# Float64 words rounded in five VectorE operations instead of seven, four places for a row of sums, and x of the gates prepared ahead of w3 @ w_out

## The chip, the cores and the metric

One Trainium2 chip, one core. The number is device time in microseconds (us) of one execution of the whole program, as a median of runs. The engines of the core are TensorE (PE, matmuls), VectorE (DVE), ScalarE (ACT), GpSimd (POOL) and SyncE (SP), whose row issues nearly all transfers between the chip's memory and the core's SBUF. Each engine works through its own row of instructions in order.

## The reference

```python
# attention: B=4, H=8, S=576, D=64; k and v averaged over groups of 8 rows
scores = scale * (q @ k_p.T);  attn = softmax(scores);  x = attn @ v_p      # -> x: 2304 x 512
# experts: E=4, hidden size F=1024, p = normalized domain_probs
for e in range(4):
    out += p[:, e:e+1] * (relu(x @ w1[e]) @ w2[e])
# gates: x = out
h = ((x @ g1) * (x @ g2)) @ w3          # 512 -> 1024, 1024 -> 1024
return h @ w_out                        # 1024 -> 512, 2304 x 512 in fp32
```

All inputs come as float64 words in memory, so a value is a pair of 32-bit words.

## The kernel before

Products need more than one fp32 pass of TensorE, so each operand is kept as a high part (rounded to fp32r) and the low rest, and `mm3` does three matmuls for one product (L170 to L172: high x low, low x high, high x high). `hi_lo` makes the two parts: ACT writes the high one (L175), DVE or POOL subtracts (L176).

The work goes in stages: the attention and a lead (to about 40 us), expert 0 in units (to 279), experts 1 to 3 with four batches each of 576 tokens (to 871), the product w3 @ w_out (to 925), and the gated part (to 1205). Expert 0 runs in units of one block of 384 tokens and one chunk of 128 hidden columns: `expert_h` makes a hidden chunk (DVE at L665), `accumulate` multiplies a block's four sums by p (L680), and `weights_of(j)` (L742 to L745 and L176) prepares the weights of the next expert's hidden product j between them. `at_pairs` says at which unit each is called.

A batch of experts 1 to 3 (`batch`) has a hidden part, `hidden(j)` for j = 0 to 3, each of seven products (`seven`, a scheme of seven products for eight) of 288 columns into banks `s`, with sums on DVE at L925, and then a second product in two halves g = 0, 1 of eight steps k (one per hidden chunk, four `mm3` of 288 columns each; step = 8g + k). At the end of each half four multiplies on DVE (L1225, out of PSUM into `part`, times p as `pb`) and four adds on POOL (L1226, into `acc`) take the sums away. Between the steps other work is called: splits of the next expert's weights (`stream.split`), its `weights_of`, and `round_some(1)`. The PSUM banks are used in turn in a ring of eight (`bank_r`), so that the first product of the next batch needs a bank that the multiplies must have emptied.

`round_some` makes one step of `Rounding`: it takes 128 x 256 float64 words of a weight matrix of the later stages, rounds them to fp32 with integer operations (L270 to L277 on DVE, L278 on POOL) and stores the result in memory (buffers `gate`, `w`, `wo`; in the trace the tiles lie in the areas `x5h` and `x5l`). There are 80 such steps, which are done with the last batch of expert 3. The step's result tile has two places, so a step waits until the store of the one two before has gone.

The stage w3 @ w_out runs as 24 units of nine or six `mm3`'s matmuls (`w_units`, weights and hidden tiles in the areas `round` and `edge`, raw words loaded as `raw<-w`), at first inside g = 1 of the last batch of expert 3 (`W3_AHEAD`). Beside it the DVE and ACT prepare x for the first gated batch (`load_x`, `prepare_x`, L758 and L871 to L874), and `put_away` stores it (`kept<-xo`, L886) so that it can be loaded again for later use.

## Time and profile before

| | |
|---|---|
| median of 3 runs | 1205.94 us (1205.91 to 1206.03) |
| profiled execution | 1207.31 us, span 1205.6 us, mean granted clock 0.994 |
| PE busy | 1171.2 us, 97% of the span |
| DVE busy | 867.4 us, 72% |
| POOL busy | 515.0 us, 43% |
| ACT busy | 366.7 us, 30% |
| moved by DMA | 222.42 MB, 184 GB/s over the span |

The median is of whole executions; the profiled execution took 1207.31, and its span is what the trace covers. Times in rows are us from the start of the span. A row of the timeline gives start, duration, engine, line, operation, the names of output and inputs, the shape, and in brackets the idle time of the engine ahead of it with what ended it. A duration of a matmul is longer than the distance to the next, since they overlap.

### The profile page before, as it was taken

Reading aid. Unit: us, or ns where it says so; the run is one execution under the profiler, and the core shown is the slowest. Engines: PE = TensorE matmul, PEld = TensorE weight load, DVE = VectorE, ACT = ScalarE, POOL = GpSimd, SP = SyncE. Lnnn points to the kernel's source line nnn. Section 1 sums busy time; section 2 is a strip of 40 time slices with the busy share of each in tenths; the row PEclk is TensorE's granted clock in tenths of the full one; section 3 lists DMA queues with packets and bytes.
Section 4 is the critical chain, followed back from the end, with each engine's and each line's share of the span. In section 5 each row is a group of like instructions: output and inputs, shape, how many; then the busy total and the mean of one; then the engine's idle time right before and its main releaser. Section 6 shows DMA issues by size and latency. Waiting matters only on the chain.

```text
span 1205.6 us, 21677 instructions
## 1 busy us (share of the span) xinstructions
PE 1171.2 (97%) x7965; PEld 1125.8 (93%) x7965; DVE 867.4 (72%) x1841; ACT 366.7 (30%) x671; POOL 515.0 (43%) x559
## 2 busy tenths in 40 slices
PE   7999999999999998999999999999989999999998
PEld 6899999999999998999999999999967999999998
DVE  7776643657777987888888778777777777785454
ACT  4533332235132134421314423032344332331010
POOL 6965122355454446654545645345310222251121
PEclk9999999999999999999999999999999999999999
DMA  8856534546665863578574565575366344845641
GB/s 211 211 139 148 173 106 148 191 163 248 225 205 179 257 176 107 167 211 257 175 221 150 164 212 177 191 267 159 128 209 220 114 160 159 331 162 208 225 182 44
DMA packets 184494, 222.42 MB, mean 184 GB/s; under 512 B 55676, under 2 KB 127428, under 8 KB 184388
## 3 DMA queue, kind: packets, MB, share of 16 engines
q1 hardware_dynamic: 184388, 221.05, 57.3%
q8 instruction: 62, 1.02, 0.3%
q14 instruction: 44, 0.36, 0.1%
HBM read 149.13 MB, written 71.86 MB: 183 GB/s over the span
## 4 chain that ended last, share of the span: by engine, by line
PE 68%; DVE 12%; DMA 8%; issue 5%; POOL 4%; ACT 2%; SPq 1%; DVEq 0%; POOLq 0%; ACTq 0%
PE g L170 11%; PE g L171 11%; PE g L172 11%; PE s L170 11%; PE s L171 10%; PE s L172 10%; DMA raw<-in_moe_w_dram 2%; PE x_ps L520 1%; POOL plain L1226 1%; DMA gate<-x5l 1%; DVE plain L925 1%; PE sc L474 1%; DVE x5l L275 1%; DMA raw<-w 1%; PE at_ps L508 1%
## 5 line engine op out<-in xcount | busy, mean ns | idle before, releaser
L176 POOL TENSOR_TENSOR round<-plain,round 128x576 fp32r<-128x576 f32 x128 | 186.6, 1463 | 314.3 <-ACT round L175 290.0
L170 PE MATMUL g<-round,w2h 128*128 128x288 f32 (+1 forms) x960 | 292.7, 305 | 2.4 <-DVE plain L680 2.1
L171 PE MATMUL g<-round,w2l 128*128 128x288 f32 (+1 forms) x960 | 291.1, 303 | 0.0
L172 PE MATMUL g<-round,w2h 128*128 128x288 f32 (+1 forms) x960 | 291.1, 303 | 0.0
L170 PE MATMUL s<-xo,wh 128*128 128x288 f32 x840 | 249.8, 297 | 13.6 <-DVE s L1225 10.9
L172 PE MATMUL s<-xo,wh 128*128 128x288 f32 x840 | 248.6, 296 | 0.0
L171 PE MATMUL s<-xo,wl 128*128 128x288 f32 x840 | 248.1, 295 | 0.0
L170 PEld LDWEIGHTS g<-round,w2h 128*128 128x128 f32 x960 | 180.5, 188 | 3.8 <-DVE plain L680 2.4
L925 DVE TENSOR_TENSOR plain<-s,plain 128x288 f32<-128x288 f32 x320 | 134.0, 452 | 67.0 <-PE s L172 33.8
L171 PEld LDWEIGHTS g<-round,w2l 128*128 128x128 f32 x960 | 180.6, 188 | 0.0
L172 PEld LDWEIGHTS g<-round,w2h 128*128 128x128 f32 x960 | 180.6, 188 | 0.0
L170 PEld LDWEIGHTS s<-xo,wh 128*128 128x128 f32 x840 | 158.4, 189 | 15.9 <-DVE s L1225 12.3
L172 PEld LDWEIGHTS s<-xo,wh 128*128 128x128 f32 x840 | 158.5, 189 | 0.0
L171 PEld LDWEIGHTS s<-xo,wl 128*128 128x128 f32 x840 | 158.1, 188 | 0.2
L175 ACT ACTIVATE round<-plain 128x576 fp32r<-128x576 f32 x132 | 89.7, 682 | 161.8 <-DVE plain L1253 158.8
L278 POOL TENSOR_TENSOR x5l<-x5l 128x256 f32<-128x256 f32 x80 | 58.9, 736 | 173.6 <-DVE x5l L277 166.1
L1159 ACT ACTIVATE plain<-plain 128x576 f32<-128x576 f32 x96 | 65.3, 680 | 158.6 <-DVE plain L925 157.0
L927 ACT ACTIVATE plain<-s 128x288 f32<-128x288 f32 x80 | 31.7, 397 | 238.2 <-PE s L172 238.0
L925 DVE TENSOR_TENSOR plain<-s,pb 128x288 f32<-128x288 f32 x160 | 67.8, 455 | 15.5 <-PE s L172 5.8
L665 DVE SCALAR_TENSOR_TENSOR round<-g,round 128x384 fp32r<-128x384 f32 x48 | 26.5, 553 | 66.3 <-ACT round L664 66.2
L170 PE MATMUL g<-xl,round 128*128 128x384 f32 x192 | 66.2, 345 | 0.0
L172 PE MATMUL g<-xh,round 128*128 128x384 f32 x192 | 64.3, 335 | 0.0
(234 smaller groups left out, 2252.2 us busy)
## 6 DMA issues: line engine op xcount, KB each, us to landing
xo<-keptx SPq DMA_DIRECT2D x72, 504.0 KB
raw<-in_moe_w_dram SPq DMA_DIRECT2D x64, 256.0 KB
x5h<-in_moe_w_dram SPq DMA_DIRECT2D x64, 256.0 KB
plain<-acc SPq DMA_DIRECT2D x12, 1152.0 KB
acc<-plain SPq DMA_DIRECT2D x12, 1152.0 KB
keptx<-xo SPq DMA_DIRECT2D x16, 576.0 KB
kept<-xo SPq DMA_DIRECT2D x12, 576.0 KB
xo<-kept SPq DMA_DIRECT2D x10, 576.0 KB
```

The source lines that it names most:

```text
L170: nc.tensor.matmul(ps, lh, rl, start=first, stop=False)
L171: nc.tensor.matmul(ps, ll, rh, start=False, stop=False)
L172: nc.tensor.matmul(ps, lh, rh, start=False, stop=last)
L175: nc.scalar.activation(hi, src, AF.Copy)
L176: (lo_eng or nc.vector).tensor_tensor(lo, src, hi.bitcast(F32), op=ALU.subtract)
L275: nc.vector.scalar_tensor_tensor(au, au, 0x7FFFFFFF, bu, op0=ALU.bitwise_and, op1=ALU.bitwise_or)
L278: nc.gpsimd.tensor_tensor(a, a, b, op=ALU.add)
L474: nc.tensor.matmul(sc[off:off + n, (hp % 2) * W:(hp % 2 + 1) * W], qT[:, hp, off:off + n], kT_t[b][:, hp * W:(hp + 1) * W], start=True, st ...
L665: nc.vector.scalar_tensor_tensor(hl, ps, 0.0, hh.bitcast(F32), op0=ALU.max, op1=ALU.subtract)
L925: nc.vector.tensor_tensor(to, one, two, op=ALU.add)
L927: nc.scalar.activation(x, product(j, A11, B11), AF.Copy)
L1159: nc.scalar.activation(r, r, AF.Relu)
```

## The change

The rounding step's arithmetic is done in five DVE operations and a POOL add of 32-bit integers instead of seven and an fp32 add, on three tiles instead of two for words that are only stored; its calls lie at other places of the hidden part (j = 1 and 3 instead of 2) and of the second product. The multiplies' results have four places (two rings and the halves of one `c` tile) instead of a ring of two. In the last batch of experts 1 and 2 the loads of the next expert's weights are issued after j = 2 instead of after the hidden part, and its `weights_of` and splits are called at earlier steps. x of the first gated batch is loaded and prepared inside the second product of the last batch of expert 3, instead of in the w3 stage, and `put_away` is called at w units 4 and 8 instead of 14 and 18. Three w units instead of two are prepared in g = 1, the hidden tiles have six places, and the w units' sums take banks of `bank_r`. `weights_of(1)` of expert 1 is called at unit 42 instead of 41.

```diff
@@ -99,0 +100,6 @@
+        def halves(self, ahead):
+            base, at = self.spots[(self.turn + ahead) % len(self.spots)]
+            size = self.spots[1][1] - self.spots[0][1]
+            return [(base, at), (base, at + size // 2)]
@@ -238 +244 @@
-            self.todo, self.loaded, self.done, self.steps = [], [], None, 0
+            self.todo, self.loaded, self.done, self.steps, self.tag = [], [], None, 0, None
@@ -240,2 +246,2 @@
-        def add(self, src, sink):
-            self.todo.append((src, sink))
+        def add(self, src, sink, tag="store"):
+            self.todo.append((src, sink, tag))
@@ -245 +251 @@
-                src, sink = self.todo.pop(0)
+                src, sink, tag = self.todo.pop(0)
@@ -251 +257 @@
-                self.loaded.append((r, sink))
+                self.loaded.append((r, sink, tag))
@@ -265,2 +271,5 @@
-            r, sink = self.loaded.pop(0)
-            t = dec.tile([P, 2, HALF], F32, tag="dtmp", name="dtmp")
+            r, sink, tag = self.loaded.pop(0)
+            if tag != self.tag:
+                self.flush()
+                self.tag = tag
+            t = dec.tile([P, 2, HALF], F32, tag=tag)
@@ -274,5 +283,3 @@
-            nc.vector.tensor_scalar(au, au, 3, 0x40000000, op0=ALU.logical_shift_left, op1=ALU.bitwise_xor)
-            nc.vector.scalar_tensor_tensor(au, au, 0x7FFFFFFF, bu, op0=ALU.bitwise_and, op1=ALU.bitwise_or)
-            nc.vector.tensor_scalar(bu, au, 0xFF800000, None, op0=ALU.bitwise_and)
-            nc.vector.scalar_tensor_tensor(b, l, 2.0 ** -52, b, op0=ALU.mult, op1=ALU.mult)
-            nc.gpsimd.tensor_tensor(a, a, b, op=ALU.add)
+            nc.vector.scalar_tensor_tensor(au, au, 3, bu, op0=ALU.logical_shift_left, op1=ALU.bitwise_xor)
+            nc.vector.tensor_scalar(b, l, 2.0 ** -51, 2.0, op0=ALU.mult, op1=ALU.add)
+            nc.gpsimd.tensor_tensor(au, au, bu, op=ALU.add)
@@ -316 +323 @@
-                rounding.add(words[i * P:(i + 1) * P, 2 * c:2 * (c + HALF)], lambda t, i=i, c=c: sink(t, i, c))
+                rounding.add(words[i * P:(i + 1) * P, 2 * c:2 * (c + HALF)], lambda t, i=i, c=c: sink(t, i, c), "turn")
@@ -845 +852 @@
-            dec = Places(din=row(x5[0], 0, 2048, 3), dtmp=row(x5[1], 0, 2048, 2), turned=row(x5[1], 4096, 1024, 2))
+            dec = Places(din=row(x5[0], 0, 2048, 3), store=row(x5[1], 0, 2048, 3), turn=row(x5[1], 0, 2048, 2), turned=row(x5[1], 4096, 1024, 2))
@@ -849 +856,2 @@
-                                   pb=Ring(p_area, [HALF_ROW]), acc=Ring(plain, [0]), **xuv)
+                                   pb=Ring(p_area, [HALF_ROW]), acc=Ring(plain, [0]), xr=Ring(x5[1], [0]),
+                                   t=Ring(x5[0], [0]), **xuv)
@@ -854 +862 @@
-            ring = row(areas["x1h"], 0, HT, 4)
+            ring = row(areas["x1h"], 0, HT, 4) + row(round_, beyond + 2 * EXTRA, HT, 2)
@@ -862 +869,0 @@
-            late["xo_ring"].turn = 0
@@ -996 +1003 @@
-        at_pairs = {38: 0, 41: 1, 46: 2}
+        at_pairs = {38: 0, 42: 1, 46: 2}
@@ -1012,3 +1018,0 @@
-                if n == LAG + 1:
-                    for kc in range(2):
-                        load_x(acc_d, 0, kc)
@@ -1018,0 +1023 @@
+        first_x = []
@@ -1023,10 +1028,2 @@
-        places = {}
-        for kc, steps in enumerate(((7, 8, 10), (13, 14, 15))):
-            for m, n in enumerate(steps):
-                def piece(kc=kc, m=m):
-                    if m == 0:
-                        places[kc] = slot()
-                    prepare_x(kc, places[kc], kept_d[0][kc], m)
-                early.setdefault(n, []).append(piece)
-        for n in (14, 18):
-            early[n].append(put_away)
+        for n in (4, 8):
+            early.setdefault(n, []).append(put_away)
@@ -1074 +1071 @@
-        W3_AHEAD = {5: 0, 6: 1}
+        W3_AHEAD = {4: 0, 5: 1, 6: 2}
@@ -1112 +1109 @@
-                        pss[:] = [bank_p("g2") for _ in range(n_out)]
+                        pss[:] = [(bank_p if u[0] == "e" else bank_r)("g2") for _ in range(n_out)]
@@ -1172 +1169 @@
-                some = j == 2 or last and not end and j == 1
+                some = j in (1, 3) and n
@@ -1183,0 +1181,6 @@
+                if j == 2 and last and not end:
+                    for m in range(NJ):
+                        add_pair(e + 1, m)
+                    for fc in turn_of:
+                        add_w2(e + 1, fc)
+                    stream.fill()
@@ -1188,6 +1191,2 @@
-            elif last:
-                for j in range(NJ):
-                    add_pair(e + 1, j)
-                for fc in turn_of:
-                    add_w2(e + 1, fc)
-                stream.fill()
+            two = small.rings["part"].spots[:2]
+            places = two + small.rings["c"].halves(1)
@@ -1194,0 +1194,2 @@
+                if end and g:
+                    places = two + two
@@ -1212,3 +1213,3 @@
-                        if step in (1, 4, 7, 10):
-                            weights_of((step - 1) // 3)
-                        if step >= 2 * FC - AHEAD:
+                        if step in (1, 3, 5, 7):
+                            weights_of(step // 2)
+                        if 0 <= step - FC - 1 < AHEAD:
@@ -1218 +1219 @@
-                    if step in (1, 3, 5, 7) and (end or not last) or step in (9, 10, 12) and not last:
+                    if step in (1, 3, 5, 7, 9, 11, 12) and not last:
@@ -1220,3 +1221,10 @@
-                    if end and step == 8:
-                        rounding.flush()
-                        assert rounding.finished()
+                    if end:
+                        if step == 0:
+                            assert rounding.finished()
+                            late["xo_ring"].turn = 0
+                            first_x.extend(slot() for _ in range(2))
+                        for kc, at in enumerate((1, 6)):
+                            if step == at:
+                                load_x(acc_d, 0, kc)
+                            if 2 <= step - at < 5:
+                                prepare_x(kc, first_x[kc], kept_d[0][kc], step - at - 2)
@@ -1224 +1232,2 @@
-                    part = small.tile([P, HB], F32, tag="part")
+                    base, at = places[d]
+                    part = base[:, at // 4:at // 4 + HB]
```

On DVE, in expert 0 around unit 42, before; `g` and `wl` are a PSUM bank and the low part of a weight:

```order
L665 SCALAR_TENSOR_TENSOR round<-g_2506,round 128x384
L176 TENSOR_TENSOR xo<-plain,xo 128x1152
L742 TENSOR_TENSOR s<-raw 128x256
L743 TENSOR_TENSOR s<-s,raw 128x256
L744 TENSOR_TENSOR s<-raw 128x256
L745 TENSOR_TENSOR s<-raw,s 128x256
L176 TENSOR_TENSOR wl<-raw,wh 128x512
L176 TENSOR_TENSOR wl<-raw,wh 128x256
L680 TENSOR_TENSOR plain<-g_2272,pb 128x384
L680 TENSOR_TENSOR plain<-g_2273,pb 128x384
L680 TENSOR_TENSOR plain<-g_2274,pb 128x384
L680 TENSOR_TENSOR plain<-g_2275,pb 128x384
```

and after:

```order
L672 SCALAR_TENSOR_TENSOR round<-g_2506,round 128x384
L182 TENSOR_TENSOR xo<-plain,xo 128x1152
L687 TENSOR_TENSOR plain<-g_2272,pb 128x384
L687 TENSOR_TENSOR plain<-g_2273,pb 128x384
L687 TENSOR_TENSOR plain<-g_2274,pb 128x384
L687 TENSOR_TENSOR plain<-g_2275,pb 128x384
L672 SCALAR_TENSOR_TENSOR round<-g_2541,round 128x384
L749 TENSOR_TENSOR s<-raw 128x256
L750 TENSOR_TENSOR s<-s,raw 128x256
L751 TENSOR_TENSOR s<-raw 128x256
L752 TENSOR_TENSOR s<-raw,s 128x256
L182 TENSOR_TENSOR wl<-raw,wh 128x512
```

The four multiplies of a block (L680, now L687) and one hidden chunk stand ahead of `weights_of(1)` (L742, now L749) and not behind it.

On DVE, in the second product of the last batch of expert 1, where `w2l` is the low part of the next expert's w2, before:

```order
L1225 TENSOR_TENSOR s<-g_4858,pb 128x288
L1225 TENSOR_TENSOR pb<-g_4859,pb 128x288
L1225 TENSOR_TENSOR s<-g_4860,pb 128x288
L1225 TENSOR_TENSOR pb<-g_4861,pb 128x288
L742 TENSOR_TENSOR s<-raw 128x256
L743 TENSOR_TENSOR s<-s,raw 128x256
L744 TENSOR_TENSOR s<-raw 128x256
L745 TENSOR_TENSOR s<-raw,s 128x256
L176 TENSOR_TENSOR wl<-raw,wh 128x512
L176 TENSOR_TENSOR wl<-raw,wh 128x256
L176 TENSOR_TENSOR w2l<-raw,w2h 128x512 x5
L1225 TENSOR_TENSOR s<-g_5020,pb 128x288
```

and after:

```order
L749 TENSOR_TENSOR s<-raw 128x256
L750 TENSOR_TENSOR s<-s,raw 128x256
L751 TENSOR_TENSOR s<-raw 128x256
L752 TENSOR_TENSOR s<-raw,s 128x256
L182 TENSOR_TENSOR wl<-raw,wh 128x512
L182 TENSOR_TENSOR wl<-raw,wh 128x256
L1234 TENSOR_TENSOR s<-g_4818,pb 128x288
L1234 TENSOR_TENSOR pb<-g_4819,pb 128x288
L1234 TENSOR_TENSOR plain<-g_4820,pb 128x288
L1234 TENSOR_TENSOR plain<-g_4821,pb 128x288
L182 TENSOR_TENSOR w2l<-raw,w2h 128x512 x5
L1234 TENSOR_TENSOR s<-g_4998,pb 128x288
```

The fourth `weights_of` stands ahead of the multiplies of g = 0 (L1225, now L1234), and these write to four places (`s`, `pb`, and twice into `plain`) instead of to two.

On SP, which issues transfers, in the w3 stage, where `raw` are words of w3, `gate` of the gates and `kept` is x put away. Before, one of two places with four stores each:

```order
L193 DMA raw<-w_120 128x384 x6
L725 DMA plain<-gate_102 128x4x128
L725 DMA plain<-gate_103 128x4x128
L193 DMA raw<-w_120 128x256 x2
L886 DMA kept<-xo 128x864
L886 DMA kept<-xo 128x1152
L886 DMA kept<-xo 128x864
L886 DMA kept<-xo 128x1152
L193 DMA raw<-w_120 128x256 x3
L725 DMA plain<-gate_102 128x4x128
L725 DMA plain<-gate_103 128x4x128
L193 DMA raw<-w_120 128x256
```

and after, in one place with all eight:

```order
L199 DMA raw<-w_120 128x384 x4
L1236 DMA acc<-plain 512x1x576
L199 DMA raw<-w_120 128x384
L893 DMA kept<-xo 128x864
L893 DMA kept<-xo 128x1152
L893 DMA kept<-xo 128x864
L893 DMA kept<-xo 128x1152
L893 DMA kept<-xo 128x864
L893 DMA kept<-xo 128x1152
L893 DMA kept<-xo 128x864
L893 DMA kept<-xo 128x1152
L199 DMA raw<-w_120 128x384 x2
```

The eight stores now stand behind the raw load of w unit 7 and ahead of those of units 8 and 9; before, the first four stood behind eleven more raw loads of w units, and the other four behind a further four.

## Rows read from the trace of the kernel before

**Rows 1.** Waits of TensorE: what waited, for what, us in all, times, longest.

```profile
PE s L170 <- DVE s L1225: 10.9, 5, 3.0
PE s L170 <- DVE pb L925: 2.7, 2, 1.5
PE g L170 <- DVE plain L680: 2.1, 1, 2.1
```

**Rows 2.** Timeline of TensorE, the first matmul behind three stops of the first kind.

```profile
332.85 0.40 PE L170 MATMUL s<-xo,wh 128*128 128x288 f32 x1 [2.13 <-DVE s L1225]
...
481.53 0.40 PE L170 MATMUL s<-xo,wh 128*128 128x288 f32 x1 [3.03 <-DVE s L1225]
...
678.23 0.40 PE L170 MATMUL s<-xo,wh 128*128 128x288 f32 x1 [2.25 <-DVE s L1225]
```

**Rows 3.** Windows: stretch, length, busy PE, PEld, DVE, ACT, POOL, PEclk, DMA, GB/s.

```profile
250.00:254.00 4.00, 3.78 (x13) 3.78 (x14) 2.02 (x5) 0.00 (x0) 2.07 (x2) 0.57 0.70 244
333.00:337.00 4.00, 4.00 (x30) 3.93 (x31) 2.62 (x7) 0.00 (x0) 3.28 (x5) 1.00 0.00 0
482.00:486.00 4.00, 4.00 (x21) 4.00 (x20) 3.09 (x8) 0.43 (x1) 2.64 (x4) 0.57 0.04 14
```

**Rows 4.** Rounding by line: ns min/median/max, first and last start; DVE's wait ahead of L270.

```profile
L276 DVE TENSOR_SCALAR x5l<-x5l x80: 293/294/1407, 297.4 to 856.3; 128x256 uint32<-128x256 uint32 x80
...
L277 DVE SCALAR_TENSOR_TENSOR x5l<-x5h,x5l x80: 424/426/428, 297.7 to 856.6; 128x256 f32<-128x256 uint32 x80
...
L278 POOL TENSOR_TENSOR x5l<-x5l x80: 725/736/787, 298.2 to 857.1; 128x256 f32<-128x256 f32 x80
...
  DMA gate<-x5l: 13.1, 9
```

**Rows 5.** Timeline of DVE, first operation of two rounding steps that follow each other.

```profile
768.93 0.50 DVE L270 TENSOR_SCALAR x5l<-x5h 128x256 uint32<-128x256 uint32 x1
...
771.94 0.29 DVE L270 TENSOR_SCALAR x5l<-x5h 128x256 uint32<-128x256 uint32 x1
```

**Rows 6.** Last batch of expert 1: timeline of DVE, then the chain of waits.

```profile
469.60 0.46 DVE L1225 TENSOR_TENSOR s<-g,pb 128x288 f32<-128x288 f32 x1 [2.45 <-POOL plain L1226]
...
474.39 1.81 DVE w2l L176
...
476.22 3.45 DMA raw<-in_moe_w_dram
```

**Rows 7.** Expert 0's end: timeline of POOL and of TensorE.

```profile
256.12 2.81 POOL L816 TENSOR_TENSOR plain<-xh,xl 128x768 f32<-128x768 f32 x2
...
277.37 0.45 PE L170 MATMUL g<-round,w2h 128*128 128x384 f32 x1 [0.33 <-DVE round L665]
```

**Rows 8.** Timeline of TensorE: first matmul of the w3 stage, first of the gates.

```profile
871.11 0.39 PE L170 MATMUL g<-round,wx 128*128 128x512 f32 x1
...
924.79 0.29 PE L170 MATMUL s<-xo,wh 128*128 128x288 f32 x1
```

**Rows 9.** The chain of waits through the w3 stage: start, us, what.

```profile
874.02 2.33 POOL plain L1226 x3
...
880.19 0.44 PE g L172
...
895.66 0.23 PE g L170
...
914.16 6.95 DMA raw<-w
```

**Rows 10.** w3 stage: transfer issues of 900 to 925, SP's timeline, windows as in rows 3.

```profile
kept<-xo SPq DMA_DIRECT2D x4, 576.0 KB
...
911.05 3.02 SPq L886 DMA_DIRECT2D kept<-xo  x4
...
846.00:858.50 12.50, 12.50 (x97) 12.50 (x96) 11.46 (x26) 2.62 (x4) 6.49 (x7) 1.00 0.20 63
904.00:909.00 5.00, 5.00 (x24) 4.14 (x23) 4.97 (x11) 3.17 (x7) 0.00 (x0) 1.00 1.04 403
```

## The prediction

> **What bounds the kernel now.** I read the page's busy times first: TensorE is busy for 97% of the span, so only two things can make the kernel shorter, TensorE's idle stretches and the stretches at half its clock. The list of waits on TensorE's own row names the idle stretches, and the timeline around each names its length [rows 1, 2]. Behind the lead of 40 us there are three families. Five stops of 10.9 us, the first hidden product of a batch (`s`) waiting for a multiply at L1225: 2.13 at 332.85, 3.03 at 481.53, 2.25 at 678.23, so 3.5 for the other two (at 729 and 778). Two stops of 2.7 at L925, where DVE sums are late because a rounding step stands ahead of them. One of 2.1 at L680. The w3 @ w_out stage runs from 871.11 to 924.79, 53.7 us [rows 8]; its 64 products of three matmuls at 0.23 [rows 9] need 64 x 3 x 0.227 = 43.6, so 10 us of it are stalls and half clock. The gated stage behind it has no stop, so what is won before its start is won in the total.
>
> The windows tell what a stop costs besides its length [rows 3]: after the 3.03 the granted clock was 0.57 over four us (1.2 GHz for most of them, so 4.0 x 0.43 = 1.7 us lost), after the 2.1 at 250 too; after the 2.13 at 332.85 it stayed 1.00. Behind the first stop of the w3 stage a matmul at 880.19 takes 0.44 where one at 895.66 takes 0.23 [rows 9]; I count another 1.7 there.
>
> **The rounding, seven operations to five, and four `part` places.** Durations by form [rows 4]: a TS takes 0.294, an STT 0.426. Gone are two TS; the last STT becomes a TS (2 x 0.294 + 0.132 = 0.72 us, of 5 x 0.294 + 2 x 0.426 = 2.32). A step in the second product lasts 3.01 [rows 5], since some operations stretch to 0.9 or 1.4 while POOL works (maximum of L276, [rows 4]). In 9 places DVE waits for a store's transfer before it rounds, 13.1 us in all [rows 4]; three store tiles instead of two move that wait one step later. A step then takes 3.01 - 0.72 = 2.3 or less. In the second product of a plain batch five to seven steps stood ahead of the last multiplies, so DVE comes 5 x 0.72 = 3.6 to 5 us earlier to them, against stops of 1.2 to 2.3; and the third and fourth multiply no longer wait for POOL's adds (2.45 in one place [rows 6]). New step places (1, 3 in the hidden part; up to 12 in the second product) only spread the same 80 steps. I put the three stops at 332.85, 729 and 778 at zero: 2.13 + 3.5 = **-5.6**. Bound on the other side: they return whole if a step does not shrink. The two L925 stops came where two rounding steps stood in neighbouring j; they are at j = 1 and 3 now and each 0.7 shorter: **-2.7** (from 0).
>
> The add on POOL changes from fp32 to uint32. The row is 0.736 [rows 4]; no row has the integer form. It is bounded by the same bytes below (0.736) and by what POOL can bear above: POOL is busy for about half of a batch of 48 us (6.49 of 12.5 in the window of [rows 10]) with 6 to 9 such adds, so it becomes the bound only at some 0.736 + 25/9 = 3.5 us each. I take 0.736, the row of the same shape. The Trainium skill, "GPSIMD Engine Reference", section "Engine selection", says that the cores add 32-bit integers natively; it gives no time, and no run here shows one yet.
>
> **The last batch of experts 1 and 2 (stops at 481.53 and 678.23).** The chain of waits [rows 6]: the third multiply of g = 0 waits 2.45 for POOL and the fourth a little; the fourth `weights_of` stands behind them, the splits of w2 behind that; the first split (474.39, 1.81) frees its buffer, the raw load issued at 476.22 takes 3.45, and behind its split stand the last multiplies, for which TensorE waits until 481.53. After the change `weights_of` stands ahead of g = 0's multiplies and these do not wait for POOL, which takes 2.7 us out of the chain: the first split ends at 476.2 - 2.7 = 473.5, the load comes 3.45 later at 477.0, and TensorE can go 1.86 behind it, as before (481.53 less 479.67), at 478.85; it wants to at 481.53 - 3.03 = 478.5. So a stop of 0.4 (0 to 1.5), and the 1.7 of half clock goes: 3.03 + 1.7 - 0.4 = **-4.3** (0 to -4.7). At 678.23 I count the stop alone, **-2.25** (0 to -2.25).
>
> **`weights_of(1)` of the gates' expert 1, from unit 41 to 42.** The accumulation of block 4 moves ahead of it on DVE, so the 2.1 stop at 250 and its half clock (1.7) go, 3.8 us. But the stretch behind is paced by a chain that TensorE is no part of: POOL's L816 at 256.12, then DVE, ACT, and at 277.37 TensorE is released [rows 7]. POOL comes to L816 at about 255.7, so 0.4 us are kept; TensorE stands for 3.7 us ahead of 277 instead. A 3.03 us stop dropped the clock in [rows 3]; if this one does, 1.7 is lost: -0.4 + 1.7 = **+1.3** (from -3.8 if the chain moves with TensorE, to +1.5).
>
> **The w3 stage.** x of gated batch 0 is prepared in the second product of the last batch. That costs DVE two times four sums and four splits, some 7 us; the four rounding steps (11 us) that stood there are gone, and DVE was 11.46 of 12.5 busy with three of them [rows 10], so I cost it at nothing. The w3 stage loses this work from DVE and ACT, and unit 0 stands ahead of g = 1's end with three units prepared. Let T be the end of g = 1 with unit 0 in it, 2.04 behind 871.11. Units 1 and 2 run to T + 4.1. Unit 3 needs `edge`, free when POOL's adds are through (before, the last three of them ended at 876.35, 5.2 behind 871.11 [rows 9]; now DVE comes to its multiplies at once, and four adds of 0.8 with the last multiply make about T + 4.3): with ACT's and DVE's split of the weights behind it a stop of about 0.9, and no half clock.
>
> Then the queue. SP's row now has all eight `kept` stores in one piece ahead of the raw loads of units 8 and 9: four of 576 KB [rows 10] and four of 864/1152 of that, 4.13 MB. At 403 GB/s, the rate of the 904 to 909 window with such stores [rows 10], this is 10.2 us. Before, with four of them from 911.05, the raw load issued behind at 914.16 was 6.95 in coming [rows 9, 10]: 10.1 us behind the first store's issue. Four more stores make it 10.1 + 5.1 = 15.2. The first store goes out at about T + 6.0 (POOL's end, and acc's store of 1.18 MB and one raw load to issue ahead; their bytes add up to 1 us): landed at T + 22, ready T + 22.6. TensorE wants unit 8 at T + 15.3 (seven units of 2.04, the 0.9 and a little). A stop of about 7.5 (5 to 9), and behind it half clock, 1.7. I keep 0.45 for a stop at the third column block, and 0.25 for each stop, by which the matmul ahead of it drains. Sum: 43.6 + 0.9 + 7.5 + 0.45 + 0.7 + 1.7 = 54.9 against 53.7: **+1.2** (-8 to +3).
>
> The Trainium skill, "DMA: Bandwidth & Descriptors", section "Where 436 GB/s comes from", says that between HBM and SBUF the HBM side binds, at about 358 GB/s per core. The trace's 403 is above it, so the trace is used; by the page's figure the stores would take 11.5 us, an estimate, and the stop would be 1.3 longer.
>
> **Sum.** -5.6 - 2.7 - 4.3 - 2.25 + 1.3 + 1.2 = -12.35. The profiled execution took 1207.31, 1.37 above the median of 1205.94; its gaps are used as differences: 1207.3 - 12.35 = 1195.0, and 1205.94 - 12.35 = **1193.6** as a median.
>
> **Rivals.** (A) The raw loads of units 8 and 9 are not held up: the stores come earlier, or transfers of a later issue pass them. Then the stage is 43.6 + 0.9 + 0.45 + 0.5 = 45.5, 9.4 below 54.9: **1184**. Against it is the 6.95 above; for it that the four stores there met other loads already queued. 0.22. (B) The last batches of experts 1 and 2 keep their stops, because the raw load and not DVE decides: 6.55 comes back, **1200**. For it is that 3.45 of DMA lies in the chain and stays there; against it that fewer loads are left behind it. 0.16. (C) Other sign: the integer add on POOL is slow. From 3.5 us each POOL is the bound of a batch; at 4.5, a batch with 9 of them takes 9 us longer on POOL than TensorE has, and over eight batches with roundings this is tens of us; just beyond the point, with 1.5 us in nine batches, 1193.6 + 14 = **1208**. Nothing in the profile speaks for it but that no row has the form. 0.07. (D) DVE's shortening is no gain at the stops, since what ends last there is POOL or a transfer: -5.6 - 2.7 vanish and the +1.2 grows to +3: **1204**. 0.05.
>
> **How the numbers follow.** The forecast case has 0.50 with a range of its own of 1190 to 1197 (the 250 term and the stop at unit 8). Likeliest time 1193.6. Range 1184 to 1201: it takes in A and B, leaves C, D and the edges out. A measurement here tells 0.2% (2.4 us) from no change. Faster: 0.50 + 0.22 + 0.16 + 0.02 of D = 0.90, less 0.02 for an unseen cost; same 0.05; slower 0.07.
>
> **What would show it.** In the profile of the changed kernel: no L1225 (now L1234) stop at the starts of batches but one of under 1 us at about 478; no stop for L925 (now L932); half clock gone behind 250 and 482, and a stop of some 3.7 ahead of 277; in the w3 stage one stop of 5 to 9 us for a raw load, some 17 us into it, with SP's eight stores ahead; POOL's add (L285) at 0.74. It is wrong if the stop at unit 8 is absent or far longer, if that at 277 moves with TensorE, or if the uint32 add is several times 0.74.

## The result and the profile after

The changed kernel takes 1193.46 us in the median of four runs (1192.54 to 1193.74), the kernel before 1205.99 (1205.91 to 1206.58) beside it: ratio 0.9894, interval [0.9877, 0.9911], 12.5 us less. The forecast was 1193.6. The profiled execution took 1193.33 with a span of 1191.5, against 1207.31 and 1205.6 before; the spans differ by 14.1, since the one profiled before was 1.4 above its median.

The waits of TensorE in the changed kernel, to be held against [rows 1] (what waited, for what, us in all, times, longest):

```profile
PE g L176 <- ACT round L181: 6.8, 1, 6.8
...
PE g L176 <- DVE round L672: 3.6, 2, 1.9
...
PE g L176 <- ACT edge L181: 1.0, 1, 1.0
PE g L177 <- DVE round L182: 0.5, 1, 0.5
```

No row for L1234 (L1225 before), L932 (L925) or L687 (L680) is left: 15.7 us of stops have gone, one of 6.8 for raw words has come, and at L672 (L665) 3.6 in two pieces stand where 0.3 stood.

Cut at four marks of TensorE's timeline (first matmul of expert 0, first `s` of expert 1, first matmul of w unit 0, first `s` of the gates), the two spans compare so. In the changed kernel unit 0 stands ahead of the last step of g = 1; the 12 matmuls of that step (1.6 us) are counted with the batches in both columns.

| stretch | before | after | difference | forecast |
|---|---|---|---|---|
| ahead of expert 0 | 27.76 | 29.23 | +1.47 | 0 |
| expert 0 | 251.80 | 251.99 | +0.2 | +1.3 |
| batches of experts 1 to 3 | 591.55 | 573.5 | -18.05 | -14.85 |
| w3 @ w_out | 53.68 | 55.9 | +2.2 | +1.2 |
| gates | 280.81 | 280.8 | 0 | 0 |

The first row is code that the change does not touch; over all profiles of this study it lies between 27.8 and 29.2, and expert 0 between 250.8 and 253.9 in kernels whose code there is alike. So 1 to 2 us of a single profile are no finding there, and a time counted from the span's start is shifted by as much; a mark nearer to the change is needed, and the section on the end of expert 0 uses one. The batches repeat within 1 us and the gates within 0.2.

**The rounding.** Two steps that follow each other, timeline of DVE, and the rows of the last two operations by line (ns min/median/max):

```profile
312.02 0.29 DVE L279 TENSOR_SCALAR x5l<-x5h 128x256 uint32<-128x256 uint32 x1
312.23 0.85 DVE L280 TENSOR_SCALAR x5l<-x5h 128x256 uint32<-128x256 uint32 x1
...
313.98 0.28 DVE L279 TENSOR_SCALAR x5l<-x5h 128x256 uint32<-128x256 uint32 x1
```

```profile
L284 DVE TENSOR_SCALAR x5l<-x5h x80: 293/294/1412, 311.8 to 817.1; 128x256 f32<-128x256 uint32 x80
...
L285 POOL TENSOR_TENSOR x5l<-x5l x80: 729/737/819, 312.2 to 817.5; 128x256 uint32<-128x256 uint32 x80
```

A step takes 1.96 (312.02 to 313.98) where [rows 5] have 3.01. The integer add on POOL takes 737 ns, the fp32 add of the same shape 736 [rows 4]: rival C had no ground. The Trainium skill, "GPSIMD Engine Reference", section "Engine selection", says that the cores add integers natively; the trace agrees in so far as the add takes no longer than the fp32 one, 737 ns.

**The last batch of expert 1**, timeline of DVE:

```profile
467.12 1.02 DVE L182 TENSOR_TENSOR wl<-raw,wh 128x512 fp32r<-128x512 f32 x2
468.06 0.45 DVE L1234 TENSOR_TENSOR s<-g,pb 128x288 f32<-128x288 f32 x1
...
468.79 0.81 DVE L1234 TENSOR_TENSOR plain<-g,pb 128x288 f32<-128x288 f32 x2
469.52 5.68 DVE L182 TENSOR_TENSOR w2l<-raw,w2h 128x512 fp32r<-128x512 f32 x5
```

The four multiplies follow each other without the 2.45 of [rows 6], and the five splits run in one piece: no raw load is waited for between them.

**The end of expert 0**, timeline of POOL, then of TensorE:

```profile
256.41 1.29 POOL L182 TENSOR_TENSOR w2l<-raw,w2h 128x512 fp32r<-128x512 f32 x1
257.66 2.81 POOL L823 TENSOR_TENSOR plain<-xh,xl 128x768 f32<-128x768 f32 x2
```

```profile
266.38 0.44 PE L176 MATMUL g<-xl,round 128*128 128x384 f32 x1 [1.63 <-DVE round L672]
...
279.00 0.45 PE L176 MATMUL g<-round,w2h 128*128 128x384 f32 x1 [1.95 <-DVE round L672]
```

The 3.6 us ahead of expert 1 are there, but in two pieces. The changed kernel's profile is already late when it comes to this part (1.47 us at the first matmul of expert 0), so times are better counted from the first operation of `weights_of(0)`, which stands at unit 38 in both kernels. That operation on DVE, and the first matmul of the second product of expert 1's first batch, before and after:

```profile
234.20 0.42 DVE L742 TENSOR_TENSOR s<-raw 128x256 f32<-128x256 f32 x1
...
301.91 0.30 PE L170 MATMUL g<-round,w2h 128*128 128x288 f32 x1
```

```profile
236.25 0.42 DVE L749 TENSOR_TENSOR s<-raw 128x256 f32<-128x256 f32 x1
...
303.56 0.30 PE L176 MATMUL g<-round,w2h 128*128 128x288 f32 x1
```

Counted so, POOL reaches L816 after 21.92 us before (256.12 of [rows 7]) and L823 after 21.41 now, 0.5 earlier, though a piece of `weights_of(1)` stands directly ahead of it; two later runs with unit 41 have 21.23 and 21.58, so 0.4 is near the spread. The stretch between the two rows takes 67.71 before, with the stop at 250 and half clock in it, and 67.31 now, with the two stops and no half clock.

**The w3 stage.** SP's timeline, the chain of waits, and the windows (stretch, length, busy PE, PEld, DVE, ACT, POOL, PEclk, DMA, GB/s):

```profile
862.26 0.52 SPq L1236 DMA_DIRECT2D acc<-plain  x1
...
863.50 10.08 SPq L893 DMA_DIRECT2D kept<-xo  x8
874.00 2.06 SPq L199 DMA_DIRECT2D raw<-w  x2
```

```profile
874.00 5.06 DMA raw<-w
...
879.74 0.80 PE g L176
...
882.41 0.43 PE g L178
...
885.38 0.23 PE g L176
```

```profile
866.00:873.00 7.00, 6.97 (x31) 5.45 (x29) 2.22 (x4) 0.94 (x3) 0.00 (x0) 1.00 1.02 402
873.00:879.70 6.70, 0.00 (x0) 0.00 (x0) 0.00 (x0) 0.52 (x1) 0.00 (x0) 0.65 1.01 361
879.70:884.00 4.30, 4.26 (x10) 3.18 (x11) 3.39 (x6) 2.51 (x5) 0.00 (x0) 0.50 0.75 248
```

The eight stores go out from 863.50 and occupy SP for 10.08 us at 402 GB/s; the raw words of unit 8 are issued at 874.00 and land at 879.06, and from 873 to 879.7 TensorE and DVE do nothing while the DMA is full. The clock falls during the stop (0.65) and is 1.2 GHz (0.50) until about 885.2: the 12 matmuls from 879.74 to there take 5.46 instead of 12 x 0.227 = 2.72, so 2.7 are lost.

### The profile page after: what moved, and what is told of

It reads as the page before. It is cut to its first block, busy times and chain, and to the rows that moved or that the text cites. A ratio compares the mean times of both kernels' runs of the same rounds, so it can differ in the third digit from the quotient of the medians.

```text
span 1191.5 us, 21553 instructions
## 1 busy us (share of the span) xinstructions
PE 1166.5 (98%) x7965; PEld 1124.3 (94%) x7965; DVE 804.8 (68%) x1681; ACT 368.9 (31%) x671; POOL 519.3 (44%) x559
## 4 chain that ended last, share of the span: by engine, by line
PE 88%; DVE 4%; DMA 2%; issue 2%; POOL 1%; ACT 1%; SPq 1%; DVEq 0%; POOLq 0%; ACTq 0%
PE g L176 16%; PE g L177 16%; PE g L178 16%; PE s L176 13%; PE s L178 12%; PE s L177 12%; PE x_ps L527 1%; PE sc L481 1%; DMA raw<-in_moe_w_dram 1%; PE at_ps L515 1%; SPq L893 1%; POOL plain L823 1%; DMA raw<-w 0%; DMA stxh<-in_k_dram 0%; DMA raw<-wo 0%
## 5 line engine op out<-in xcount | busy, mean ns | idle before, releaser
L932 DVE TENSOR_TENSOR plain<-s,plain 128x288 f32<-128x288 f32 x320 | 138.4, 452 | 88.9 <-PE s L178 67.4
L285 POOL TENSOR_TENSOR x5l<-x5l 128x256 uint32<-128x256 uint32 x80 | 59.1, 738 | 117.0 <-DVE x5l L284 114.5
L934 ACT ACTIVATE plain<-s 128x288 f32<-128x288 f32 x80 | 32.2, 402 | 250.9 <-PE s L178 250.6
L932 DVE TENSOR_TENSOR plain<-s,pb 128x288 f32<-128x288 f32 x160 | 69.8, 455 | 24.3 <-PE s L178 15.0
L672 DVE SCALAR_TENSOR_TENSOR round<-g,round 128x384 fp32r<-128x384 f32 x48 | 26.5, 553 | 62.1 <-ACT round L671 61.9
```

Of the source, the lines that this page charges most:

```text
L285: nc.gpsimd.tensor_tensor(au, au, bu, op=ALU.add)
L672: nc.vector.scalar_tensor_tensor(hl, ps, 0.0, hh.bitcast(F32), op0=ALU.max, op1=ALU.subtract)
L932: nc.vector.tensor_tensor(to, one, two, op=ALU.add)
L934: nc.scalar.activation(x, product(j, A11, B11), AF.Copy)
```

## The experiments

All are the changed kernel with one edit (b_41, b_43 and b_44 are s_half with one), and each ratio is to the kernel before on the same chip, so they are compared by ratio with the 0.9894 of the changed kernel; where the differences are small, the stretches of the traces tell more. The runs were on three chips, and there the kernel before spread from 1203 to 1211. A stretch is of the one profiled execution of a run, which can lie off its median.

**Where the eight stores stand: s_four, s_half, s_late, s_48.**

```diff
# s_four (put_away itself, so also in the gates)
-            for f in stores:
+            for f in stores[:4]:
                 f()
-            stores.clear()
+            del stores[:4]
-        for n in (4, 8):
+        for n in (14, 18):
```

> The changed kernel with its eight kept stores put away as before, four at w unit 14 and four at unit 18. Theory 1 (the eight stores in one piece hold up the raw words of unit 8): the 6.77 us stop at 879.74 and the half clock behind it (879.7 to 885.3, some 2.8 us) go, about 9.5 us, and a small stop of 1 to 2 us at the later units may come; 1184.5 (1183 to 1187). Rival (unit 8 is late for another reason, the load on ACT and DVE or raw loads issued late): the stop stays within 2 us of 6.77, 1192 to 1194.

This kernel issues four stores at every later put-away too, where eight are due, so the gates work on x that is in part not stored. 1183.83, ratio 0.9794 [0.9771, 0.9817]; w3 stage 46.9 (48.49 less the 1.6). The next one does the same to the first eight alone:

```diff
+        def put_half():
+            for f in stores[:4]:
+                f()
+            del stores[:4]
-        for n in (4, 8):
-            early.setdefault(n, []).append(put_away)
+        for n in (14, 18):
+            early.setdefault(n, []).append(put_half)
```

> The changed kernel with the first eight kept stores put away in halves at w units 14 and 18, as before, and all later ones as changed. Theory (the eight stores in one piece at unit 4 hold up the raw words of unit 8): no stop over 1 us and no half clock in the w3 stage, 9.5 us less than the changed kernel, ratio to before 0.982 (0.980 to 0.984). Rival (the stop comes from the load on ACT and DVE): ratio 0.988 to 0.990.

1182.59 (1182.0 to 1183.2), ratio 0.9789 [0.9768, 0.981]. Timeline of TensorE in the w3 stage of s_half, all its stops:

```profile
859.65 0.50 PE L176 MATMUL g<-round,edge 128*128 128x512 f32 x1 [1.15 <-ACT edge L181]
...
893.28 0.50 PE L177 MATMUL g<-round 128*128 128x512 f32 x1 [0.77 <-DVE round L182]
...
896.61 0.50 PE L176 MATMUL g<-round,edge 128*128 128x512 f32 x1 [0.36 <-ACT edge L181]
```

The 6.77 stop and the half clock are gone; the stage takes 47.5, 8.4 less than in the changed kernel. By ratio it is 12.7 us less, more than expected; another 2.3 of the profile lie ahead of expert 1, where the edit changes nothing, and the rest is not settled. The 1.15 stop was not expected either, and the changed kernel has it as 1.05. That raw words wait behind the stores in SP's row is shown: DVE and ACT do the same work in both.

```diff
# s_late: all eight at unit 14
-        for n in (4, 8):
+        for n in (14,):
# s_48: put_half of s_half, at units 4 and 8
+        for n in (4, 8):
+            early.setdefault(n, []).append(put_half)
```

> The changed kernel with all eight kept stores still in one piece, but at w unit 14. Theory 1a (the length of the piece decides wherever it stands): the stop moves to the units whose raw words are issued behind it, 4 to 7 us with half clock behind a long stop, 1190 (1187 to 1193). Theory 1b (the place decides, since by unit 14 more raw words are already loaded ahead and the piece is hidden): no stop over 2 us, 1185 (1183 to 1187).

1188.12, ratio 0.9825 [0.9798, 0.9852]. Timeline of TensorE, the stop behind the stores:

```profile
895.29 0.50 PE L176 MATMUL g<-round,edge 128*128 128x512 f32 x1 [3.23 <-ACT edge L181]
```

> The changed kernel with the kept stores in halves at w units 4 and 8. Theory (the stop grows with the bytes ahead: 5.1 us less of stores ahead of unit 8's words): the 6.8 us stop becomes 1 to 2.5 us without half clock, and a second one of 0 to 3 at the units behind unit 11; 1185.5, ratio to before 0.981 to 0.985. Rival (any store ahead of unit 8 holds its words up as long): the stop stays over 5 us, ratio 0.987 or more.

1187.12, ratio 0.9835 [0.9813, 0.9856]. Timeline of TensorE in s_48:

```profile
872.76 0.49 PE L176 MATMUL g<-round 128*128 128x512 f32 x1 [1.17 <-ACT round L181]
...
883.42 0.50 PE L176 MATMUL g<-round,edge 128*128 128x512 f32 x1 [1.28 <-ACT edge L181]
```

In s_late the same piece moves the stop to a later unit and halves it, with half clock behind: both theories were half right, the length decides and a later place hides part of it. In s_48, 2.06 MB less ahead of unit 8's words make 6.77 into 1.17, 5.6 us, where 2.06 MB at 402 GB/s are 5.1. s_late's stage takes 50.8 and s_48's also 50.8, between 47.5 and 55.9.

**The step's length: r_seven.**

```diff
-            nc.vector.scalar_tensor_tensor(au, au, 3, bu, op0=ALU.logical_shift_left, op1=ALU.bitwise_xor)
-            nc.vector.tensor_scalar(b, l, 2.0 ** -51, 2.0, op0=ALU.mult, op1=ALU.add)
-            nc.gpsimd.tensor_tensor(au, au, bu, op=ALU.add)
+            nc.vector.tensor_scalar(au, au, 3, 0x40000000, op0=ALU.logical_shift_left, op1=ALU.bitwise_xor)
+            nc.vector.scalar_tensor_tensor(au, au, 0x7FFFFFFF, bu, op0=ALU.bitwise_and, op1=ALU.bitwise_or)
+            nc.vector.tensor_scalar(bu, au, 0xFF800000, None, op0=ALU.bitwise_and)
+            nc.vector.scalar_tensor_tensor(b, l, 2.0 ** -52, b, op0=ALU.mult, op1=ALU.mult)
+            nc.gpsimd.tensor_tensor(a, a, b, op=ALU.add)
```

> The changed kernel with the rounding in the old seven operations of DVE and an fp32 add, the rest as changed. Theory (the shorter step took the three stops of plain batches): a step is about 1 us longer (3.0 for 1.95), seven of them in a second product make DVE up to 7 us later against a slack of 2.7 to 5.6, so stops of 1 to 3 us return in three to six batches, +6 (3 to 12), 1199.5. Rival (four places for the sums and the new step places took them): +0 to +1.5, 1193.5 to 1195.

1205.52, ratio 0.9978 [0.9964, 0.9992]; batches 15.3 us longer than in the changed kernel. Two of its nine stops there, timeline of TensorE, and a window behind the second:

```profile
403.95 0.40 PE L176 MATMUL g<-round,w2h 128*128 128x288 f32 x1 [1.53 <-DVE pb L934]
...
631.02 0.61 PE L176 MATMUL s<-xo,wh 128*128 128x288 f32 x1 [3.55 <-DVE s L1236]
```

```profile
631.00:635.00 4.00, 3.98 (x16) 3.98 (x17) 3.53 (x9) 0.96 (x2) 3.46 (x5) 0.50 0.01 2
```

By ratio 10.1 us more than the changed kernel, within the range that I gave; the profiled execution was the slowest of ten, and its 15.3 are more. There are stops at the multiplies (L1236 there) in four batches, 5.6 us, five more where the sums of the hidden part (L934) come late, 4.6 us, which I had not expected, and the clock at 1.2 GHz behind the longest. With the old step the new calls cost more than the old ones did: two hidden steps in each batch but an expert's first, where most batches of the kernel before have one. The stops do not stand where they stood: none is at the three plain batches that had one before (332.85, 729, 778), and the two plain ones are at 578 and 631. Ahead of each of those three, DVE of the kernel before waited for a store's transfer, timeline of DVE:

```profile
318.61 0.29 DVE L270 TENSOR_SCALAR x5l<-x5h 128x256 uint32<-128x256 uint32 x1 [3.67 <-DMA wo<-x5l]
...
714.52 0.30 DVE L270 TENSOR_SCALAR x5l<-x5h 128x256 uint32<-128x256 uint32 x1 [2.92 <-DMA gate<-x5l]
...
763.90 0.30 DVE L270 TENSOR_SCALAR x5l<-x5h 128x256 uint32<-128x256 uint32 x1 [3.68 <-DMA gate<-x5l]
```

r_seven, which keeps the third store tile, has no such wait in those second products; the changed kernel has some (2.28 at 321.71, 2.52 at 325.72) and no stop behind them. So the third tile is a rival to the shorter step for these three stops, and no run takes it back.

**Four places: p_two; the moves in the last batches: l_late.**

```diff
# p_two
-            places = two + small.rings["c"].halves(1)
+            places = two + two
```

> The changed kernel with two places for the multiplies' results instead of four, so that the third multiply waits for POOL again. Theory (in plain batches the 1.2 us of waiting lie inside a slack of 2.7 us or more, in the last batches of experts 1 and 2 the 2.7 us lie in the chain and the slack there is about 0.8): two stops of 1 to 2 us, one perhaps with half clock, +3 (1.5 to 6), 1196.5. Rival (the places carry the whole gain of the stops at L1225): stops return in five batches, +8 to +11, 1202 to 1204.

1202.02, ratio 0.9947 [0.9918, 0.9976], by ratio 6.4 us more than the changed kernel; batches 9.1 longer, 0.6 of it half clock behind the stop ahead of expert 1. Timeline of DVE in the last batch of expert 1, of TensorE behind it, and the windows behind the two stops:

```profile
472.02 0.46 DVE L1234 TENSOR_TENSOR s<-g,pb 128x288 f32<-128x288 f32 x1 [2.46 <-POOL plain L1235]
...
478.70 0.69 DVE L182 TENSOR_TENSOR w2l<-raw,w2h 128x512 fp32r<-128x512 f32 x1 [2.22 <-ACT w2h L181]
```

```profile
479.81 0.40 PE L176 MATMUL s<-xo,wh 128*128 128x288 f32 x1 [2.88 <-DVE s L1234]
...
674.96 0.40 PE L176 MATMUL s<-xo,wh 128*128 128x288 f32 x1 [2.30 <-DVE s L1234]
```

```profile
480.00:484.00 4.00, 4.00 (x22) 4.00 (x22) 2.93 (x8) 0.15 (x1) 2.93 (x4) 0.65 0.01 2
675.00:679.00 4.00, 4.00 (x19) 4.00 (x20) 2.94 (x8) 0.01 (x1) 3.07 (x4) 0.60 0.08 30
```

The place was right and the size was not: stops in the last batches of experts 1 and 2 alone, but 5.2 with half clock behind both (4 x 0.35 + 4 x 0.40 = 3.0), not 3. The 2.46 for POOL turns into a wait of 2.22 for the last raw words further on, as in [rows 6]. In plain batches the third multiply waits for POOL, up to 0.9, and nothing comes of it.

```diff
# l_late
-                if j == 2 and last and not end:
-                    for m in range(NJ):
-                        add_pair(e + 1, m)
-                    for fc in turn_of:
-                        add_w2(e + 1, fc)
-                    stream.fill()
             settle()
...
+            elif last:
+                for m in range(NJ):
+                    add_pair(e + 1, m)
+                for fc in turn_of:
+                    add_w2(e + 1, fc)
+                stream.fill()
...
-                        if step in (1, 3, 5, 7):
-                            weights_of(step // 2)
-                        if 0 <= step - FC - 1 < AHEAD:
+                        if step in (1, 4, 7, 10):
+                            weights_of((step - 1) // 3)
+                        if step >= 2 * FC - AHEAD:
```

> The changed kernel with the next expert's loads of the last batch issued behind the hidden part again, its weights_of at steps 1, 4, 7, 10 and its splits at 11 to 15. Theory (four places carry most of the gain at 481 and 678, since with two the stops came back at 2.9 and 2.3): stops of 0 to 1.5 us in the two last batches, 2 more (0 to 4), ratio 0.991. Rival (the moves carry it as much, either alone is not enough): stops of 2 to 3 us with half clock, 6 to 9 more, ratio 0.9945 to 0.997.

1199.95, ratio 0.9922 [0.9891, 0.9953]; batches 9.2 longer, 0.7 of it half clock as in p_two, and stops of 3.43 and 1.79. Timeline of DVE ahead of the first, then of TensorE:

```profile
478.71 0.69 DVE L182 TENSOR_TENSOR w2l<-raw,w2h 128x512 fp32r<-128x512 f32 x1 [1.64 <-ACT w2h L181]
```

```profile
479.82 0.40 PE L176 MATMUL s<-xo,wh 128*128 128x288 f32 x1 [3.43 <-DVE s L1234]
```

By the trace my theory of this run fell: four places do not carry most of it. By ratio the run is 3.4 us above the changed kernel, within -0.4 and +7.1, which does not tell the theory from the rival; its executions go from 1195.99 to 1202.61, and the profiled one is the slowest. In the two traces either edit alone leaves the two stops whole, since in both the last split waits for words that were loaded too late (ACT's `w2h`, for which DVE waits, comes from them); only together they remove them.

**The hidden steps' places: j_12.**

```diff
-                some = j in (1, 3) and n
+                some = j in (1, 2) and n
```

> The changed kernel with the hidden part's rounding steps at j = 1 and 2 instead of 1 and 3. Theory (neighbouring steps overload DVE in the hidden part): stops at L932 of 1 to 1.5 us in two to six batches, 3 more (1.5 to 6), ratio 0.992. Rival (the shorter step alone is enough): within 1 us of the changed kernel, ratio 0.989 to 0.990.

1193.35, ratio 0.9877 [0.9854, 0.9899]; batches 0.7 longer, which is half clock behind the stop ahead of expert 1, and no stop at L932. The rival holds: with the shorter step, neighbouring j's do no harm.

**Where `weights_of(1)` stands: a_41, b_41, b_43, b_44.** The first is the changed kernel, the others s_half, with another unit:

```diff
-        at_pairs = {38: 0, 42: 1, 46: 2}
+        at_pairs = {38: 0, 41: 1, 46: 2}     # a_41, b_41; 43 in b_43, 44 in b_44
```

> The changed kernel with weights_of(1) at unit 41 again. Theory (the last unit of expert 0 is paced by POOL's work behind weights_of(1) and not by TensorE): the 2.1 us stop at 250 and its half clock come back, the stops at 266 and 279 shrink to about 0.3, and expert 1 begins 1.6 us earlier, as in the kernel before: 1.6 less than the changed kernel, ratio 0.988. Rival (what is won at 250 is kept): 2 to 3.8 us more, ratio 0.991 to 0.993.

1191.68, ratio 0.9861 [0.9837, 0.9885]. The rival (0.991 to 0.993) is out, and the theory's 0.988 lies inside the interval; the stop at 250 is back and those ahead of expert 1 are gone.

> The changed kernel with the kept stores in halves at units 14 and 18 and weights_of(1) at unit 41. Theory (stops at 266 and 279 come from POOL's work of weights_of(1) being late and cost 3.6; the stop at 250 with its half clock costs 3.8): no different from s_half by more than 1 us, ratio to before 0.978 to 0.980. Rival (the move to 42 was a loss of 1.6 or more): 1.5 to 2.5 us less than s_half, ratio 0.977.

1181.94 (1181.53 to 1182.77), ratio 0.9788 [0.9769, 0.9807], not to be told from s_half's 0.9789. One stop, with 0.79 of the clock over the eight us behind it in both; timeline of TensorE in b_41:

```profile
249.72 0.44 PE L176 MATMUL g<-round,w2h 128*128 128x384 f32 x1 [2.06 <-DVE plain L687]
```

> The same with weights_of(1) at unit 43. Theory (POOL then comes to L823 without weights_of(1)'s pieces ahead, so the chain to the last unit is some 1.6 us earlier, while accumulate of block 4 is still ahead on DVE): the stops at 266 and 279 shrink from 3.6 to 0 to 2 us, 2 us less than s_half, ratio 0.977 (0.975 to 0.979). Rival (the pieces stand ahead of the last unit wherever they are): 0 to 2 us more than s_half.

1184.76, ratio 0.9812 [0.9792, 0.9832]. Timeline of TensorE in b_43:

```profile
277.35 0.45 PE L176 MATMUL g<-round,w2h 128*128 128x384 f32 x1 [3.55 <-DVE round L672]
```

> The same with weights_of(1) at unit 44. Theory: as at 43 for POOL's first L823, but weights_of(1) and weights_of(2) are then only two units apart, and the second is what the last unit stands behind on DVE: stops of 2 to 5 us, -1 to +2 us against s_half. Rival (DVE and ACT have room): 2 to 3.5 us less than s_half, ratio 0.976.

1186.53, ratio 0.9827 [0.9805, 0.985], stops of 1.88 at 273.30 and 2.37 at 279.22. The windows behind the stop of b_43, and behind the first of b_44:

```profile
277.30:281.30 4.00, 3.95 (x14) 3.93 (x15) 1.83 (x4) 0.79 (x2) 4.00 (x5) 0.58 0.38 124
```

```profile
273.30:277.30 4.00, 3.55 (x12) 3.04 (x12) 3.26 (x6) 2.27 (x5) 0.00 (x0) 0.60 0.59 212
```

My theory for 43 and 44 fell: the stop at 266 goes, and those ahead of expert 1 grow by as much, 3.55 and 4.25 in all for 3.6; the last unit waits for the same chain. In b_43 the idle comes in one piece, and the clock falls behind it: 4 x 0.42 = 1.7 us, which is most of the 2.2 us by which b_43 is above s_half. That it falls because the piece is one is not shown, since with two pieces it falls in some executions too. The table has the stretch of the section on the end of expert 0, from the first operation of `weights_of(0)` to the second product of expert 1's first batch, in all profiled executions; but for a rounding step in the kernel before, for which TensorE does not wait, the code there differs in the unit alone.

| unit | profiled executions | stretch | clock behind a stop |
|---|---|---|---|
| 41 | before, a_41, b_41 | 67.71, 67.17, 67.48 | 1.2 GHz for a time, in all three |
| 42 | changed kernel, s_four, s_half, s_48 | 67.30 to 67.33 | 2.4 GHz |
| 42 | s_late, r_seven, p_two, l_late, j_12 | 68.81 to 68.86 | 1.2 GHz for a time |
| 43 | b_43 | 69.09 | 1.2 GHz for a time |
| 44 | b_44 | 69.17 | 1.2 GHz for a time |

The windows behind the stop of 1.95 in the changed kernel and behind the same stop in p_two:

```profile
279.00:283.00 4.00, 4.00 (x26) 4.00 (x27) 2.13 (x4) 1.68 (x3) 4.00 (x5) 1.00 0.43 152
```

```profile
278.80:282.80 4.00, 4.00 (x16) 4.00 (x17) 2.23 (x4) 1.26 (x2) 4.00 (x5) 0.63 0.40 133
```

So unit 42 lies among the three of unit 41 where the clock stays up (0.4 under the kernel before, 0.1 over a_41), and 1.1 to 1.7 above them where it falls; b_43 is 0.3 above the executions of unit 42 in which it fell. In b_44 the half clock is 1.6 (4 x 0.40) and the longer stops 0.7, 2.3 of the 3.9 by which it is above s_half; the rest is not settled.

s_half and b_41 beat both kernels: 0.9789 and 0.9788 against 0.9894.

## Why the prediction was right

The sum was right to 0.2 us, and some of that is luck: three terms are off, by -3.2, -1.1 and +1.0 in the profile, the stretch ahead of expert 0, which I put at nothing, gave 1.5 back there, and the profile before was 1.4 above its median. The -1.1 hangs on a clock that fell in some executions and not in others.

- **The three stops of plain batches, -5.6, and the two at L925, -2.7.** Gone. At L925 the shorter step is what the runs point to: r_seven has stops of that kind at j = 1 and 3, and j_12 with the shorter step has none at neighbouring j. That it took the three of plain batches is not shown: r_seven has multiplies that come late in plain batches, but not in these three. Four places (p_two) and j = 1 and 3 (j_12) are not needed with the shorter step; the third store tile, which I had only moving a wait, was not tried alone.
- **The last batches, -4.3 and -2.25.** Gone, with the 0.4 that I had left in. The chain was right, with both of its parts needed in the traces (p_two, l_late). Rival B, that the raw load alone decides and the stops stay, is out: in the changed kernel none is left.
- **Batches together, -18.05 for -14.85: the size that was off.** I counted each stop as the idle time of its row. A stop costs more: around the stop at 332.85 [rows 2] the timeline of TensorE before has

```profile
330.42 0.30 PE L172 MATMUL s<-xo,wh 128*128 128x288 f32 x1
...
333.09 0.29 PE L171 MATMUL s<-xo,wl 128*128 128x288 f32 x1
```

So 2.67 pass over two steps from one matmul to the next that take 0.27 otherwise, 2.40 for a row of 2.13. Seven such are 7 x 0.27 = 1.9 of the missing 3.2; I had put this drain into the w3 term and left it out here. Of the rest 0.4 is the stop that I had left in the sum, and 0.9 are ten steps of 0.23 to 0.31 between matmuls (0.13 otherwise) in the kernel before, such as the one to 826.31, which the list of waits does not hold; the changed kernel has two of them.

- **`weights_of(1)`, +1.3.** The row of expert 0 has +0.2, which is within its spread; counted from `weights_of(0)` it is -0.4 (67.31 for 67.71), or +0.1 against a_41. So the 0.4 that I had as kept is no more than the spread; the idle of 3.7 is there as 3.6, though in two pieces. The half clock that I added for it was not a sure cost: it did not come in this execution, and it came in five of the nine with the same code there, in which the term is +1.1 (+1.7 against a_41). So the mechanism held, and its largest part is one that a single execution has or has not; why is open.
- **w3 stage, +1.2, was +2.2.** The first store was put at T + 6.0, with T = 856.8 here 862.8, and went out at 863.50; the words at T + 22, 878.8, and landed at 879.06; the stop at 7.5 and was 6.77. The size that was off is the half clock, 1.7 in the sum and 2.7 in the rows; the drain around the stops was 1.2 for 0.7, and the stops together 8.3 for 8.85. On the rate: the Trainium skill, "DMA: Bandwidth & Descriptors", section "Where 436 GB/s comes from", has 358 GB/s as what the side of the memory gives; the 402 of the stretch with nearly nothing but stores is above it, so the measurement decides.
- **Rival A** (1184) is what s_half shows, at 1182.6, once the stores stand elsewhere: its price was near (9.4 off the stage, and s_half has 8.4) and its condition not given.

## What to carry to other kernels

A store that nobody waits for is not free: ahead of a load in the same row it holds up the engine that waits for that load, by its bytes over the rate, less what is already loaded ahead. Where several late steps end in one wait, undo each alone before crediting any: here either of two edits by itself left both stops whole. Count from a mark close to the change, since the start of the span moves by more than the effect. And cost a stop of TensorE with what drains ahead of it, and with the clock behind it.

## What the runs showed of the hardware

The clock behind a stop of TensorE is not a matter of its length alone: 2.25 and 2.28 in the kernel before were followed by a granted clock of 1.00, 2.30 in p_two by 0.60 over four us; 1.63 and 1.95 in the changed kernel by 1.00, 1.88 in b_44 by 0.60. Nor is it fixed by the code: the same two stops were followed by 1.00 in four executions, and the second by 0.57 to 0.68 in five. Behind the 6.77 the loss was 2.7 us, not the 1.7 seen behind shorter ones. What decides it stays open. So the price of a stop of about 2 us is 2 or 4, and a forecast must hold both.
